# Channel mixing of a fused attention kernel: later loads of the second pass held to set times, planner durations a few per cent longer

## Chip, cores and metric

One NeuronCore of a Trainium2 chip runs the whole program. The metric is device microseconds (us) for one execution, lower is better. The kernel before takes 673.16 us (median of 3 runs, 673.02 to 673.44).

## Reference

Three blocks follow each other, on B=4 batches, H=8 heads, S=576 tokens, D=64, so C=512 channels and 2304 tokens.

```python
scores = where(mask, q @ k.T / sqrt(D), -1e9)   # window 32; heads 4..7 every 4th of 128
x = softmax(scores) @ v                         # B, S, C
# block 1, channel mixing
xk, xr = mu_k*x + (1-mu_k)*x_prev, mu_r*x + (1-mu_r)*x_prev
x = sigmoid(xr @ w_r) * (maximum(xk @ w_k, 0)**2 @ w_v)        # 512 -> 1024 -> 512
# block 2, token and channel mixing
u = x + (maximum(x.T @ w_tok1, 0) @ w_tok2).T                  # 576 -> 256 -> 576
out = u + maximum(u @ w_ch1, 0) @ w_ch2                        # 512 -> 1536 -> 512
```

## The kernel before

The program is written as one long list of steps (function `tile_model`), and nothing in the list is issued at once. A class `Plan` collects the steps and their dependencies, and `order` (L304) then plays them through in planned time: every step has a duration from `_cost` (L258), a due time that is worked back from the PE step that needs it, and the engine that comes free first takes the ready step with the earliest due time. `emit` (L407) writes the instructions in that order, all from L421. This is why all rows of the profile name L421; a row is told apart by its tiles. On the chip each engine runs its instructions in that order and waits on semaphores; planned times do not exist there.

Four things steer the planner around this change:

- `_cost` gives the planned duration of a transfer (SP, SyncE's queue, issues all of them), of an ACT and of a DVE instruction.
- Copies, conversions and some scalings are written with both engines (`nc.either`, L470). The planner takes the first named one, ACT for copies, unless that would end too late; then the one that ends sooner. So durations decide which engine does them.
- `nc.hold` gives a step an earliest planned time, counted from the time that PE would reach this place of the list if it never waited. The weights of the second pass have such holds (L1264), weight conversions too (`slowly`, L836).
- `SPARE` is added to the planned landing of a load when a step of `slowly` reads it.

Precision: every fp32 product is split in a high and a low part (fp32r) and done with three matmuls (`mm3`). The large products use seven-product block forms (names A11, S1, A12, S2, S4, S3, A22), so 2x2 blocks need seven sweeps.

The part that the holds touch is the last product, `out = u + mid @ w_ch2`. A first pass wrote `mid` (1536 channels) to DRAM as `part_mid0` to `part_mid2`, one for each c of three groups of 768 tokens, and u as `part_u0` to `part_u2`. The second pass, `result(c)` (L1276), does for each c:

- `load(q)` (L1280) fetches quarter q of `part_mid` as two tiles of 128x1152 into a ring of 14 places (`half_r`: tiles wv, raw, z, at); four loads of 128x768 fetch u into `us`.
- `parts(q)` splits a tile into high and low, 128x1152 each, on ACT or DVE; `turned` and `less` form differences of tiles on DVE.
- `sweep` runs one of the seven forms on PE: two banks, 18 matmuls of 384 columns each. S2, S4, S3 and A22 add into banks that hold an earlier sum.
- `plus` empties a bank on DVE into an output tile (128x384), `send` stores it to `outT` through SP. The output tiles are a ring of three: z4, z5 (their last third) and y0.

Each c gives eight output tiles. All loads of the next c may be issued by SP as soon as their place in the ring is free; the planner puts them among the stores and weight loads by due time. Before the second pass, SP also fetches the seven weight forms from DRAM (`part_A11` to `part_A22`), which the first pass's weight conversions stored there.

The early part, for the other terms: `keys`, `receptance` and `mix` are the products with w_k, w_r and w_v of block 1, run between the attention units of the first batches.

Of the kernel before, what the change touches and what calls it, by code (L numbers as in the profile page):

```python
# [154 lines left out]
class Plan:  # L155
# [17 lines left out]
    }  # L173
    TAIL = dict(tensor=0.0, vector=0.08, scalar=0.10, gpsimd=0.0, sync=0.0)
    TICK, BUSY = 10.24 / 3, 3060
    SPARE = 3.0

    def __init__(self, nc):
        self.nc = nc
# [77 lines left out]
    @staticmethod  # L257
    def _cost(engine, method, kw):  # L258

        out = kw["out"]  # L260
        cols = int(np.prod(out.shape[1:]))
        pointers = sum(hasattr(kw.get(k), "space") for k in ("scale", "bias", "scalar", "scalar1"))
        if engine == "sync":
            if kw["in_"].dtype == U32:
                return max(0.45, 4 * cols * out.shape[0] / 230e3 - 0.9)
            return max(0.45, 8 * (0.03 + 4 * cols * 0.0266e-3))
        if engine == "tensor":
            if kw.get("is_transpose"):
                return cols / 1200 + 0.0025
            if kw["lhsT"].dtype in (F32R, BF16):  # L270
                return cols / 2263 + 0.0049
            if kw["lhsT"].shape[0] <= D or out.shape[0] <= D:
                return cols / 1200 + 0.0025
            return 2 * max(cols / 1200 + 0.0025, 0.112)
        source = kw.get("in_", kw.get("in0"))
        psum = source is not None and "PSUM" in str(source.space)
        if engine == "scalar":
            read = 0.093 * (kw.get("accum_out") is not None)
            return (0.07 if psum else 0.1) + cols / 1200 + 0.03 * pointers + read
        if engine == "gpsimd":  # L280
            return 0.04 if method == "memset" else 0.04 + cols / 345
        if method == "tensor_reduce":
            return 0.066 + int(np.prod(source.shape[1:])) / 960
        if method == "reciprocal":
            return 0.066 + cols / 157
        fast = method in ("tensor_copy", "tensor_scalar", "tensor_scalar_add") and not psum
        return 0.066 + 0.05 * pointers + cols / (1920 if fast else 960)

    def _run(self, at, cost, kw):

# [13 lines left out]
    def order(self):  # L304
# [41 lines left out]
        for _ in range(n):  # L346
# [50 lines left out]
            for s in after[i]:  # L397
                for o in self.ops[s]:
                    spare = self.SPARE if e == "sync" and s in self.floor else 0.0
                    ready[s][o] = max(ready[s][o], end + self.TAIL[e] + self.DELAY[e][o] + spare)  # L400
# [34 lines left out]
def tile_model(nc, banks, kept_k, kept_1, kept_w, kept_u, kept_mid, units, cst, mu, w_k, w_v, w_r, w_t1, w_t2, w_c1, w_c2, outT):  # L435
# [40 lines left out]
    def combine(out, in0, in1, op):  # L476
        nc.vector.tensor_tensor(out=out, in0=in0, in1=in1, op=op)

    def split(raw, hi, lo):
        copy(hi, raw)  # L480
        combine(lo, raw, f(hi), ALU.subtract)

    def rows(n):
        return slice(128 * n, 128 * n + 128)
# [264 lines left out]
    def mix(c, m, j):  # L749
# [16 lines left out]
        out=om_sb, in0=mu_sb, scalar1=-1.0, scalar2=1.0, op0=ALU.mult, op1=ALU.add  # L766
    )
    diag = []
    for kt in range(4):
        diag.append([])  # L770
        for k, factor in enumerate((om_sb, mu_sb)):
# [3 lines left out]
                    out=d, in0=ident, scalar1=factor[:, col], scalar2=None, op0=ALU.mult)),  # L775
# [68 lines left out]
    for g in range(8 * nchunk + 2):  # L844
        c, m = divmod(g, 8)
# [34 lines left out]
    def product(out, a, b, first=True, last=True, goes_on=False):  # L880
        for k, ((ah, al), (bh, bl)) in enumerate(zip(a, b)):
            mm3(out, ah, al, bh, bl, first and k == 0, last and k == len(b) - 1, goes_on)
# [377 lines left out]
    for n, (name, places) in enumerate(zip(NAMES, w2_at)):  # L1260
        start = len(nc.ops)
# [14 lines left out]
    def result(c):  # L1276
        us = [u_r.tile(2, N2) for _ in range(4)]
        quads = {}

        def load(q):  # L1280
            quads[q] = [half_r.tile(3, N2) for _ in range(2)]
            for i, t in enumerate(quads[q]):
                nc.sync.dma_start(out=t, in_=kept_mid[c][:, q, 3 * i:3 * i + 3])

        def parts(q):
            out = []
            for t in quads[q]:
                hl = tuple(hl_r.tile(3, N2, dtype=F32R) for _ in range(2))
                split(t, *hl)
                out += [tuple(v[:, k] for v in hl) for k in range(3)]  # L1290
            return out

        def less(q, other):
            for t, o in zip(quads[q], quads[other]):
                combine(t, t, o, ALU.subtract)

        def turned(q, other):
            for t, o in zip(quads[q], quads[other]):
                combine(t, o, t, ALU.subtract)

        def sweep(name, b, banks, **kw):
            for a in range(2):
                lhs = [tuple(v[:, rows(a)] for v in hl) for hl in w2[name]]
                product(banks[a], lhs, b, **kw)

        def plus(ps, others, tiles):
            for p, o, t in zip(ps, others, tiles):
                combine(t, p, o, ALU.add)

        def send(tiles, kt, half):  # L1310
            for a, t in enumerate(tiles):
                at_t = 2 * N2 * c + N2 * half
                nc.sync.dma_start(out=outT[rows(kt + a), at_t:at_t + N2], in_=t)

        def two(r):
            return [r.tile(N2) for _ in range(2)]

        def u_of(kt, half):
            return [us[kt + a][:, half] for a in range(2)]

        x, y, z = two(x_r), two(y_r), two(z_r)
        on = dict(first=False, goes_on=True)
        load(0)
        load(1)
        for kt in range(4):
            nc.sync.dma_start(out=us[kt], in_=kept_u[c][:, kt])
        load(2)
        load(3)
        sweep("A11", parts(0), x)
        s1 = two(aside_r)  # L1330
        plus(x, u_of(0, 0), s1)
        turned(0, 1)
        sweep("S1", parts(0), y)
        s5 = two(aside_r)
        plus(y, u_of(2, 1), s5)
        sweep("A12", parts(2), z)
        t = two(out_r)
        plus(z, s1, t)
        send(t, 0, 0)
        turned(0, 3)  # L1340
        sweep("S2", parts(0), x, **on)
        s2 = two(aside_r)
        plus(x, u_of(0, 1), s2)
        sweep("S4", parts(3), y, **on)
        t = two(out_r)
        plus(y, s2, t)
        send(t, 0, 1)
        less(3, 1)
        sweep("S3", parts(3), x, **on)
        t = two(out_r)  # L1350
        plus(x, s5, t)
        send(t, 2, 1)
        less(2, 0)
        sweep("A22", parts(2), x, **on)
        t = two(out_r)
        plus(x, u_of(2, 0), t)
        send(t, 2, 0)

    for c in range(3):
        result(c)  # L1360
# [88 lines left out]
```

## Time and profile before

| | |
|---|---|
| runs, median (lowest to highest) | 673.16 us (673.02 to 673.44) |
| the profiled execution | 671.81 us |
| its span, first to last instruction | 670.0 us |
| PE busy, matmuls | 653.8 us, 98%, 4105 matmuls |
| DVE busy | 566.7 us, 85%, 1188 instructions |
| ACT busy | 371.4 us, 55%, 981 instructions |
| DMA | 146.45 MB, mean 219 GB/s |
| chain that ended last | PE 72%, DVE 11%, DMA 9%, ACT 5% |

A busy time says how long an engine had an instruction in hand, averaged over stages with different limits. PE at 98% means that only 16 us of the span are free of matmuls, 7.4 us of them in the first 50 us. The chain is followed back from the last instruction, at each step to whatever released it.

### The profile page before, as it was taken

Reading aid. Unit: us, or ns where it says so; the run is one execution under the profiler, and the core shown is the slowest. Engines: PE = TensorE matmul, PEld = TensorE weight load, DVE = VectorE, ACT = ScalarE, POOL = GpSimd, SP = SyncE. Lnnn points to the kernel's source line nnn. Section 1 sums busy time; section 2 is a strip of 40 time slices with the busy share of each in tenths; the row PEclk is TensorE's granted clock in tenths of the full one; section 3 lists DMA queues with packets and bytes.
Section 4 is the critical chain, followed back from the end, with each engine's and each line's share of the span. In section 5 each row is a group of like instructions: output and inputs, shape, how many; then the busy total and the mean of one; then the engine's idle time right before and its main releaser. Section 6 shows DMA issues by size and latency. Waiting matters only on the chain.

```text
span 670.0 us, 11558 instructions
## 1 busy us (share of the span) xinstructions
PE 653.8 (98%) x4105; PEld 603.0 (90%) x4105; DVE 566.7 (85%) x1188; ACT 371.4 (55%) x981; POOL 2.1 (0%) x22
## 2 busy tenths in 40 slices
PE   6899999999999999999999999999999999899997
PEld 6678888888888888998889899999999999899997
DVE  4999998799799989777699888798898569899982
ACT  4989785789669875435278555264474122312310
POOL 0000000000000000000000000000000000000000
PEclk9999999999999999999999999999999999999999
DMA  8989444675774535713533769777697999933211
GB/s 325 385 310 331 142 126 150 190 261 166 249 237 149 198 115 179 237 38 121 164 111 133 233 193 364 275 254 256 247 356 253 413 408 412 392 107 95 71 36 59
DMA packets 65385, 146.45 MB, mean 219 GB/s; under 512 B 5808, under 2 KB 24368, under 8 KB 64304
## 3 DMA queue, kind: packets, MB, share of 16 engines
q1 hardware_dynamic: 65328, 145.72, 62.3%
q8 instruction: 32, 0.52, 0.3%
q14 instruction: 25, 0.20, 0.1%
HBM read 95.89 MB, written 49.81 MB: 217 GB/s over the span
## 4 chain that ended last, share of the span: by engine, by line
PE 72%; DVE 11%; DMA 9%; ACT 5%; issue 1%; SPq 0%; DVEq 0%; ACTq 0%
PE bank L421 72%; DVE z L421 3%; DVE at L421 2%; DVE x L421 2%; DMA z<-part_mid 2%; ACT z L421 2%; DVE wv L421 1%; ACT at L421 1%; ACT x L421 1%; DMA outT<-z 1%; DMA outT<-y 1%; DMA x<-w_k 1%; DMA wr<-units 1%; DMA part_mid<-at 1%; DMA at<-units 1%
## 5 line engine op out<-in xcount | busy, mean ns | idle before, releaser
L421 PE MATMUL bank<-z,wk 128*128 128x384 f32 x644 | 141.9, 345 | 0.3 <-ACT z L421 0.3
L421 PE MATMUL bank<-wv,z 128*128 128x512 f32 x432 | 124.3, 402 | 1.3 <-ACT raw L421 1.3
L421 PEld LDWEIGHTS bank<-z,wk 128*128 128x128 f32 x644 | 112.7, 188 | 5.7 <-ACT z L421 0.9
L421 PEld LDWEIGHTS bank<-wv,z 128*128 128x128 f32 x432 | 78.0, 188 | 14.6 <-ACT raw L421 1.6
L421 ACT ACTIVATE at<-at 128x96 f32<-128x96 f32 (+3 forms) x183 | 67.0, 369 | 36.3 <-DVE at L421 34.9
L421 ACT ACTIVATE z<-z 128x384 fp32r<-128x384 f32 (+1 forms) x90 | 46.4, 523 | 23.2 <-DVE z L421 15.7
L421 PE MATMUL bank<-xt,wk 128*128 128x384 f32 x254 | 54.0, 346 | 0.8 <-ACT at L421 0.8
L421 PE MATMUL bank<-wr,z 128*128 128x512 f32 x192 | 53.7, 406 | 1.0 <-DVE z L421 1.0
L421 PE MATMUL bank<-xt,x 128*128 128x384 f32 x248 | 48.8, 334 | 0.0
L421 PE MATMUL bank<-z,x 128*128 128x384 f32 x232 | 47.0, 334 | 0.0
L421 PEld LDWEIGHTS bank<-xt,wk 128*128 128x128 f32 x254 | 44.4, 188 | 2.6 <-issue 1.1
L421 DVE TENSOR_TENSOR z<-z,z 128x384 fp32r<-128x384 f32 (+1 forms) x78 | 44.2, 574 | 1.8 <-ACT z L421 0.6
L421 PEld LDWEIGHTS bank<-xt,x 128*128 128x128 f32 x248 | 43.5, 188 | 0.0
L421 DVE TENSOR_TENSOR at<-bank,at 128x384 f32<-128x384 f32 x64 | 35.2, 552 | 7.8 <-PE bank L421 7.2
L421 PEld LDWEIGHTS bank<-wr,z 128*128 128x128 f32 x192 | 34.3, 188 | 7.3 <-DVE z L421 1.3
L421 PEld LDWEIGHTS bank<-z,x 128*128 128x128 f32 x232 | 40.8, 188 | 0.0
L421 ACT ACTIVATE x<-bank 96x512 f32<-96x512 f32 (+1 forms) x48 | 28.1, 589 | 11.8 <-PE bank L421 11.6
L421 ACT ACTIVATE at<-bank 128x384 f32<-128x384 f32 x36 | 17.5, 488 | 27.0 <-PE bank L421 26.2
L421 DVE TENSOR_TENSOR raw<-raw 128x256 f32<-128x256 f32 (+1 forms) x76 | 30.2, 420 | 0.2
L421 PE MATMUL bank<-at 128*128 128x96 f32 (+1 forms) x121 | 22.1, 275 | 5.4 <-DMA at<-cst 5.0
L421 PE MATMUL bank<-cst,at 128*96 128x128 f32 x144 | 26.8, 274 | 0.2 <-DVE at L421 0.2
L421 PE MATMUL bank<-z,at 128*128 128x512 f32 x96 | 25.5, 397 | 0.0
(234 smaller groups left out, 1327.1 us busy)
## 6 DMA issues: line engine op xcount, KB each, us to landing
part_mid<-at SPq DMA_DIRECT2D x18, 768.0 KB, 5.9
z<-part_mid SPq DMA_DIRECT2D x11, 576.0 KB, 9.3
x<-w_c SPq DMA_DIRECT2D x12, 512.0 KB, 4.0
at<-units SPq DMA_DIRECT2D x14, 416.0 KB, 3.7
unit<-units SPq DMA_DIRECT2D x13, 416.0 KB, 3.8
at<-units SPq DMA_DIRECT2D x21, 256.0 KB, 3.4
part_w<-wv SPq DMA_DIRECT2D x21, 256.0 KB, 2.7
part_w<-x SPq DMA_DIRECT2D x21, 256.0 KB, 3.0
```

The source lines that it names most:

```text
L421: call(kw["out"], kw["constant"]) if method == "memset" else call(**kw)
```

## The change

Three constants of the planner and one earliest time are changed; what is computed, and every step of the list, stays.

```diff
-    SPARE = 3.0
+    SPARE = 2.0
...
-            return max(0.45, 8 * (0.03 + 4 * cols * 0.0266e-3))
+            return max(0.45, 8 * (0.045 + 4 * cols * 0.0266e-3))
...
-            return (0.07 if psum else 0.1) + cols / 1200 + 0.03 * pointers + read
+            return (0.08 if psum else 0.11) + cols / 1170 + 0.03 * pointers + read
...
-        return 0.066 + 0.05 * pointers + cols / (1920 if fast else 960)
+        return 0.075 + 0.05 * pointers + cols / (1860 if fast else 930)
...
-        load(0)
-        load(1)
-        for kt in range(4):
-            nc.sync.dma_start(out=us[kt], in_=kept_u[c][:, kt])
-        load(2)
-        load(3)
+        for wait, first, q in ((-5.0, 0, 0), (-5.0, 0, 1), (0.0, 1, 0), (5.0, 0, 2), (5.0, 0, 3)):
+            start = len(nc.ops)
+            if first:
+                for kt in range(4):
+                    nc.sync.dma_start(out=us[kt], in_=kept_u[c][:, kt])
+            else:
+                load(q)
+            if c:
+                nc.hold.update(dict.fromkeys(range(start, len(nc.ops)), wait))
```

So for c=1 and c=2 the first four loads may start, in planned time, 5 us before the group's first matmul, u at it, and the last four 5 us after it. The number of transfers is the same (355), and PE has the same 4105 matmuls; 164 steps that either engine can do change theirs, 85 from DVE to ACT and 79 from ACT to DVE.

SP, from the last weight loads before the second pass to its start. A name like `x21_1_4077` is a tile of the slot x21; `part_S3_82` is the DRAM copy of weight form S3. Before:

```order
L421 DMA x26_1_3686<-part_S2_80 128x1024
L421 DMA part_mid2_89<-at0_2_4184 512x1x384
L421 DMA x20_1_3889<-part_S4_81 128x2048
L421 DMA x21_1_4077<-part_S4_81 128x1024
L421 DMA at0_2_4184<-part_u0_84 128x768
L421 DMA x21_1_4077<-part_S3_82 128x1024
L421 DMA x22_3_4130<-part_S3_82 128x1024
L421 DMA x23_3_4240<-part_S3_82 128x1024
L421 DMA wr0_3_5411<-part_A22_83 128x1024
```

and now:

```order
L421 DMA z1_3_5324<-part_mid0_87 128x1152
L421 DMA part_mid2_89<-at0_2_4186 512x1x384
L421 DMA raw0_2_3330<-part_u0_84 128x768
L421 DMA x20_1_3896<-part_S4_81 128x2048
L421 DMA at0_2_4186<-part_u0_84 128x768
L421 DMA x21_1_4082<-part_S4_81 128x1024
L421 DMA part_S3_82<-y0_3_4387 128x512
L421 DMA x21_1_4082<-part_S3_82 128x1024
L421 DMA x22_3_4123<-part_S3_82 128x1024
L421 DMA x23_3_4245<-part_S3_82 128x1024
L421 DMA wr0_3_5423<-part_A22_83 128x1024
```

A load of u (raw0) and a store to part_S3 come here from further up the queue (both stood in the 13 rows above), and the other load of u now precedes x21's. In those rows, too, the loads of S1's weights (wk1, wk2, 128x1024 and 128x2048) now precede a store to part_mid2 that stood ahead of them, and x26's load precedes those of z0 and z1.

SP, the rows that follow, around the first output stores; `part_mid1_88` and `part_u1_85` are c=1's data, z4 and z5 the output tiles. Before:

```order
L421 DMA z3_1_5420<-part_mid1_88 128x1152
L421 DMA wr1_3_5431<-part_A22_83 128x1024
L421 DMA wr3_3_5442<-part_A22_83 128x1024
L421 DMA z4_2_5438<-part_mid1_88 128x1152
L421 DMA z5_2_5461<-part_mid1_88 128x1152
L421 DMA at2_2_4135<-part_mid1_88 128x1152
L421 DMA outT<-z5_2_5461 128x384
L421 DMA at0_2_4184<-part_mid1_88 128x1152
L421 DMA outT<-z4_2_5438 128x384
L421 DMA at0_2_4184<-part_mid1_88 128x1152
L421 DMA wv0_2_3622<-part_mid1_88 128x1152 x2
L421 DMA unit0_2_4088<-part_u1_85 128x768
```

and now:

```order
L421 DMA wr1_3_5434<-part_A22_83 128x1024
L421 DMA wr3_3_5446<-part_A22_83 128x1024
L421 DMA outT<-z4_2_5442 128x384
L421 DMA outT<-z5_2_5461 128x384
L421 DMA z3_1_5481<-part_mid1_88 128x1152
L421 DMA z4_2_5442<-part_mid1_88 128x1152
L421 DMA z5_2_5461<-part_mid1_88 128x1152
L421 DMA at2_2_4134<-part_mid1_88 128x1152
L421 DMA unit0_2_4088<-part_u1_85 128x768
L421 DMA unit1_2_4108<-part_u1_85 128x768
L421 DMA outT<-y0_4_5526 128x384
L421 DMA at0_2_4186<-part_mid1_88 128x1152 x2
```

The first two output stores now precede all loads of c=1, and the c=1 loads of at0 and wv0 come behind those of u and a third output store. Further on, c=2's eight loads stood before among the stores of c=0; now four of them stand behind the store of z4 that SP issued at 600.87 in the profile, and four behind the next store of z5.

PE, around the second receptance product (`wr` by z0, z1); `wv0` by z4 are the mixing products. Before:

```order
L421 MATMUL bank0_63<-at0_0_339 128x96 x4
L421 MATMUL bank3_66<-wr2_1_507,z0_0_402 128x512 x3
L421 MATMUL bank3_66<-wr3_1_516,z0_0_402 128x512 x3
L421 MATMUL bank3_66<-wr0_1_438,z1_0_493 128x512 x3
L421 MATMUL bank3_66<-wr1_1_449,z1_0_493 128x512 x3
L421 MATMUL bank1_64<-cst0_0_111,at2_0_142 96x128 x4
L421 MATMUL bank5_68<-wv0_1_597,z4_1_547 128x512 x2
```

and now:

```order
L421 MATMUL bank0_63<-at0_0_366 128x96 x4
L421 MATMUL bank5_68<-wv0_1_587,z4_1_545 128x512
L421 MATMUL bank6_69<-wv0_1_587,z4_1_545 128x512
L421 MATMUL bank7_70<-wv0_1_587,z4_1_545 128x512
L421 MATMUL bank3_66<-wr2_1_505,z0_0_466 128x512 x3
L421 MATMUL bank3_66<-wr3_1_514,z0_0_466 128x512 x3
L421 MATMUL bank3_66<-wr0_1_429,z1_0_485 128x512 x3
```

Three mixing matmuls, which came later, stand ahead of the receptance rows. On ACT, five steps of the attention now precede the first conversion of w_k, and the first conversion of w_v precedes a step of `keys` that it followed.

## Rows read from the trace of the kernel before

**Rows 1.** The page, busy time, share of the span and instructions of each engine.
```profile
PE 653.8 (98%) x4105; PEld 603.0 (90%) x4105; DVE 566.7 (85%) x1188; ACT 371.4 (55%) x981; POOL 2.1 (0%) x22
```

**Rows 2.** Stretches (us): busy of PE, PEld, DVE, ACT, POOL; granted clock, DMA share, GB/s.
```profile
0.00:50.00 50.00, 42.59 (x357) 34.94 (x357) 39.55 (x93) 38.30 (x126) 1.08 (x20) 1.00 0.91 341
50.00:100.00 50.00, 49.02 (x386) 42.65 (x388) 49.48 (x106) 43.31 (x131) 0.00 (x0) 1.00 0.60 198
...
550.00:600.00 50.00, 47.94 (x275) 47.33 (x275) 45.84 (x49) 12.95 (x12) 0.00 (x0) 1.00 0.84 324
```

**Rows 3.** Timeline, PE: start, us, engine, operation, out<-in, count [idle before <-releaser].
```profile
50.92 3.06 PE L421 MATMUL bank<-wr,z 128*128 128x512 f32 x12 [0.96 <-DVE z L421]
...
572.21 5.02 PE L421 MATMUL bank<-xt,wr 128*128 128x384 f32 x25 [1.94 <-issue]
```

**Rows 4.** Timeline, DVE, before and in the second pass; same columns.
```profile
529.80 0.56 DVE L421 TENSOR_TENSOR at<-bank,at 128x384 f32<-128x384 f32 x1 [0.54 <-PE bank L421]
...
555.64 0.55 DVE L421 TENSOR_TENSOR z<-bank,at 128x384 f32<-128x384 f32 x1
...
565.89 1.36 DVE L421 TENSOR_TENSOR xt<-z,xt 128x1152 fp32r<-128x1152 f32 x1
568.43 0.56 DVE L421 TENSOR_TENSOR z<-bank,z 128x384 f32<-128x384 f32 x1 [1.18 <-DMA outT<-z]
568.90 1.35 DVE L421 TENSOR_TENSOR xt<-z,xt 128x1152 fp32r<-128x1152 f32 x1
570.28 1.36 DVE L421 TENSOR_TENSOR z<-z,z 128x1152 f32<-128x1152 f32 x1
571.56 0.55 DVE L421 TENSOR_TENSOR z<-bank,z 128x384 f32<-128x384 f32 x1
...
575.11 0.56 DVE L421 TENSOR_TENSOR y<-bank,z 128x384 f32<-128x384 f32 x1 [0.94 <-DMA outT<-y]
```

**Rows 5.** Timeline, SP's issues of transfers, before and in the second pass; same columns.
```profile
519.96 0.52 SPq L421 DMA_DIRECT2D part_mid<-at  x1
...
557.95 0.34 SPq L421 DMA_DIRECT2D outT<-z  x1
558.33 0.43 SPq L421 DMA_DIRECT2D at<-part_mid  x1
559.01 0.34 SPq L421 DMA_DIRECT2D outT<-z  x1
560.29 0.32 SPq L421 DMA_DIRECT2D at<-part_mid  x1
561.62 1.73 SPq L421 DMA_DIRECT2D wv<-part_mid  x2
564.55 1.75 SPq L421 DMA_DIRECT2D unit<-part_u  x2
566.52 0.34 SPq L421 DMA_DIRECT2D outT<-y  x1
...
600.87 0.34 SPq L421 DMA_DIRECT2D outT<-z  x1
```

**Rows 6.** Chain of waits: start, us, what.
```profile
557.95 8.51 DMA outT<-z
...
575.72 90.79 PE bank L421 x522
```

**Rows 7.** Stretch 560 to 570; columns as in rows 2.
```profile
560.00:570.00 10.00, 10.00 (x60) 9.95 (x58) 8.76 (x11) 1.17 (x1) 0.00 (x0) 1.00 1.03 411
```

**Rows 8.** Transfers issued at 536.07 and 537.29: count, KB, us to landing.
```profile
part_mid<-at SPq DMA_DIRECT2D x1, 768.0 KB, 11.7
...
x<-part_S SPq DMA_DIRECT2D x1, 1024.0 KB, 12.9
```

**Rows 9.** Timeline, ACT, first readers of c=1's and c=2's later loads.
```profile
579.17 1.17 ACT L421 ACTIVATE xt<-at 128x1152 fp32r<-128x1152 f32 x1 [0.34 <-PE bank L421]
...
610.38 1.17 ACT L421 ACTIVATE xt<-wv 128x1152 fp32r<-128x1152 f32 x1 [5.07 <-PE bank L421]
```

**Rows 10.** Timeline, ACT, first conversion of w_k.
```profile
24.79 1.15 ACT L421 ACTIVATE x<-x 128x1024 f32<-128x1024 f32 x1 [0.79 <-DMA x<-w_k]
```

## The prediction, made before the changed kernel had run

> **What bounds the kernel.** I read the page's engine table first: PE is busy 98% of the span, DVE 85% [rows 1]. So only the places where PE stands idle can be won. The table by stretches shows where they are [rows 2]: 7.4 us in the first 50 us, 1.0 in the next 50, where DVE is busy 49.5 of 50 us, and 2.1 in the stretch from 550 to 600. The granted clock is 1.00, the 2.4 GHz level, in every one of these rows, so no term below comes from the clock. The timeline of PE puts the late loss at one point: matmuls of sweep A22 start at 572.21 after 1.94 us of idle time [rows 3]. The page names no engine for it, so I followed the banks. A22 adds into bank 0, which DVE must first empty after sweep S3. DVE's timeline [rows 4] shows it late: it waits 1.18 us for a store of an output tile, starts at 568.43, then two passes over 128x1152 and, at 571.56, the row that empties bank 0; it ends at 572.11. A second wait, 0.94 us at 575.11 for the store of y, holds A22's later half: its matmuls start at 575.72 [rows 6], where 18 from 572.21 at 0.173 each (a sweep of 36 takes 6.24) would end near 575.4, so some 0.3 more.
>
> Why is that store late? The tile is written from 555.64 to 556.19 [rows 4], yet SP issues its store at 559.01 [rows 5]. It stands behind loads of the next 768 tokens, and SP cannot issue freely: the chain of waits [rows 6] shows the z5 store of 557.95 landing after 8.51 us, at 566.46, and SP issuing the y store at 566.52. Between these two issues lie exactly seven others [rows 5]. So **SP's ninth transfer waits until the first has landed**. With DMA at 103% and 411 GB/s [rows 7], each transfer lands when the bytes before it are through: 8 to 13 us after its issue.
>
> **The change, part by part.** It adds and removes no instruction. Hold times and costs act only in the planner; on the chip they are an order.
>
> 1. *The stores of the first output tiles, ahead of the loads.* In the new SP order the stores of z4 and z5 stand in front of z3, z4, z5 and at2 for c=1. I work out the landings by bytes at that rate: 0.64 us for a 128x512 store, 1.28 for a 128x1024 load, 1.43 for 128x1152, 0.96 for 128x768, 2.55 for 128x2048, 0.48 for an output tile. The starting point is the store of part_mid issued at 536.07, which landed 11.7 us later, at 547.8 [rows 8]. Two transfers, 0.64 + 0.96 us, no longer stand ahead of it, so it lands at 546.2. Behind it follow raw 0.96, x20 2.55, at0 0.96, x21 1.28 and the moved store to part_S3 0.64: 552.6. The load of x23 waits for that landing, since it reads what was stored; three loads of S3 and three of A22 take 7.7: 560.3. The two output stores land at 560.7 and 561.2, then z3 at 562.7, z4 at 564.1, z5 at 565.5, at2 at 567.0.
> DVE needs the z4 store by the end of its row of 565.89, which takes 1.27 start to start as the next ones do: 567.16. The store has landed 6.5 us earlier, so the 1.18 us wait goes. It then needs z3 at 567.6 and z5 at 568.9; both are there, z5 with 3.4 us to spare. Bank 0 is emptied from 570.2 to 570.8, 1.3 us sooner, and A22 starts at about 570.85. **What is late next** is DVE itself: PE could start at 570.27, so 0.6 of the 1.94 stays. The y store now lands near 569.4, before DVE's 573.8, so the 0.3 goes as well. Gain 1.3 + 0.3 = 1.6 us. The bounds: both stalls vanish, 2.2, or the work behind takes it all back, 0.
> 2. *Loads of c=1 and c=2 later.* The loads at +5 of c=1 (at0, wv) land by about 575, before the first row that reads them, ACT's of 579.17 [rows 9]. For c=2 the first four now stand behind stores of c=1, the last of them the one issued at 600.87 [rows 5]. They issue from 601.3 and land by bytes at 604.1 to 608.4; the first reader, ACT, started at 610.38 [rows 9]. Cost 0; the cover is 4 us or more, and each us beyond it would be a us of PE.
> 3. *SP before the second pass.* Loads of S1's weights pass the part_mid store of 519.96 [rows 5]: 1.57 MB less the raw load's 0.39 ahead of it, 2.9 us later, at 530.4. DVE's next write into that buffer was at 529.80 [rows 4], so DVE may wait 0.6. PE has other banks there: taken 0, bound 0.6. One weight load (x26, 1.28) now precedes the z0 and z1 loads, against 1.6 us taken away: 0.3 earlier, taken 0.
> 4. *The early order.* PE's three mixing matmuls (wv by z4, 512 columns) move ahead of the receptance row at 50.92, where it stood idle 0.96 [rows 3]. Twelve took 3.06 there, so three fill 0.7 or so. But on ACT the conversion of w_v, 128x1024 like ACT's row of 24.79 [rows 10] and so 1.0 us to the next start, now stands ahead of the step that this receptance row waits for through DVE: 1.0 later. Net +0.3; bounds -0.7 and +1.0. On ACT the first conversion of w_k waited 0.79 us for its load [rows 10]; five attention steps now fill that and 1.2 us more. Taken 0, since attention is that much further on; bounds -0.8 and +1.2.
> 5. *Engines.* By the new costs 85 steps go from DVE to ACT and 79 back; casts of 128x384 on DVE fall from 26 to 18, copies of it rise from 19 to 26. From 50 to 100, where DVE is the bound, PE has 1.0 idle to give back; I take half, -0.5, bounds -1.0 and +1.0 (one more wait like the one at 50.92). Between 100 and 550 PE idles little and DVE and ACT have room: 0, bounds of 1 either way.
>
> Sum: -1.6 + 0.3 - 0.5 = **-1.8 us**. The profiled execution took 671.81 (span 670.0 and 1.81 around it), so it would take 670.0; the runs' median, 673.16, is 1.35 above that execution, so I forecast 671.4.
>
> How much cover item 1 has hangs on the rate, 411 GB/s in the row. The Trainium skill, "DMA: Bandwidth & Descriptors", section Specifications, gives a limit of about 358 GB/s of HBM for each core; by it (an estimate from that page) the 7.9 MB from 546.2 to the landing of z5 would take 22.1 instead of 19.3 us, z5 would land at 568.4, half a us before its use, and the sum would be the same with its cover gone. The trace does not agree here; the measured rate stands.
>
> **The rivals.**
> *Nothing left (about 673.2).* The second pass gains its 1.6, and the early order loses as much: +1.0 at the receptance row and +0.6 of the 1.2 at w_k's conversion, with DVE too full from 50 to 100 to make it up. For it: those are the stretches with least slack. Against: PE's early idle time is mostly elsewhere. It is also the case in which the holds don't bind: nothing keeps SP from issuing on the chip but the order, and if DVE's own backlog alone set 572.21, earlier stores would change nothing. The 1.18 us in DVE's row speaks against that.
> *Slower by the moved store to part_S3 (675.5).* All weights of A22, both output stores and the loads of c=1 stand behind x23, which waits for this store. I have it issued at 547.2 and landing 5.4 us later. The store of 536.07 took 11.7 us and the load of 537.29 took 12.9 [rows 8]. z5 lands 12.9 us behind the store and A22 starts 1.95 us behind z5, so with a landing at 557.9 (10.7 us) the whole gain of item 1 is gone; from there each us is a us of PE. At 13.0 us z5 lands at 573.1, A22 starts at 575.0, 2.8 late, less 0.3 and 0.2 for the rest: +2.3. For it: the rows. Against: little is queued ahead at 547 (raw and x20, 3.5 us).
> *More than that (669.5).* The second pass gains the full 2.2, because DVE's run from 543 starts 0.3 earlier, and the early stretch gives 1.5 from the idle time above.
>
> **How the numbers follow.** Forecast case 0.5, nothing left 0.25, slower 0.15, more 0.1. A measurement of this kernel tells 0.2%, 1.35 us, from no change. The forecast and the larger gain count as faster (0.6), nothing left as the same (0.25), the rest as slower (0.15). The range takes in the larger gain with half a us, 669.0, and above 673.9, nothing left with 0.7 more from part of the bounds of items 3 to 5; the slower case stays outside.
>
> **What would show it.** Right: no wait for a store in DVE's row near 567; A22 starting near 570.9 with some 0.6 us of idle time, none 3.5 us later; SP issuing the z4 store at about 556.2; no wait for a load after 600. Wrong: an x23 load issued much after 552.6 or DVE waiting for z5 (the slower case); a wait of more than 1 us before the receptance row near 51, or PE's first 100 us longer than before by over 1 (nothing left).

## The result, and the profile after

Four runs of the changed kernel took 664.48 us in the median (664.06 to 664.57), four of the kernel before beside them 673.25 (673.02 to 673.44): ratio 0.987, 95% interval 0.985 to 0.989. The gain is 8.8 us where 1.8 was forecast, below the range. The profiled execution took 664.45 with a span of 662.7, so the spans differ by 7.3.

The page of the kernel after, busy time by engine, which answers to [rows 1]:

```profile
PE 651.1 (98%) x4105; PEld 603.0 (91%) x4105; DVE 562.1 (85%) x1182; ACT 379.4 (57%) x987; POOL 2.1 (0%) x22
```

PE does the same 4105 matmuls in 2.7 us less busy time and stands idle 4.6 us less. Stretches of the kernel before that the prediction did not show, with the columns of [rows 2]:

```profile
100.00:150.00 50.00, 49.61 (x337) 44.21 (x333) 42.39 (x113) 34.55 (x122) 0.00 (x0) 1.00 0.62 199
150.00:200.00 50.00, 48.73 (x356) 42.78 (x355) 44.42 (x123) 38.79 (x133) 0.00 (x0) 1.00 0.69 216
250.00:300.00 50.00, 49.92 (x257) 45.12 (x256) 41.86 (x95) 23.77 (x54) 0.00 (x0) 1.00 0.48 158
```

The same of the kernel after, with those of [rows 2] but the first:

```profile
50.00:100.00 50.00, 49.91 (x395) 43.46 (x394) 49.23 (x109) 45.20 (x137) 0.00 (x0) 1.00 0.64 216
100.00:150.00 50.00, 50.00 (x358) 44.56 (x358) 43.44 (x121) 35.87 (x128) 0.00 (x0) 1.00 0.62 197
150.00:200.00 50.00, 50.00 (x351) 44.74 (x348) 44.56 (x121) 38.73 (x127) 0.00 (x0) 1.00 0.73 229
...
550.00:600.00 50.00, 49.75 (x287) 49.46 (x286) 47.72 (x53) 12.88 (x11) 0.00 (x0) 1.00 0.66 243
```

PE is nearly gapless from 50 us on. But the table also hides something: between 100 and 550 the idle time falls only from 2.2 to 0.4 us, and PE got 3.9 ahead there. The rest does not show as idle time, since the ends of the matmuls are modelled: at token mixing, for one, idle time falls by 0.1 us, while 0.65 us less lies in distances from one matmul's start to the next that are 0.1 to 0.2 us longer than usual. So I compared starts: the matmul with the same number in both traces, at places where PE has done the same work in both. (The next matmul need not be the same one; at 50.92 it is the receptance row before and a mixing product after.)

| place in the program | before | after | earlier by |
|---|---|---|---|
| first attention work | 16.48 | 16.45 | 0.0 |
| before the receptance row of [rows 3] | 50.92 | 49.59 | 1.3 |
| block 1 | 100.41 | 99.08 | 1.3 |
| after the wait at 147 | 147.09 | 145.18 | 1.9 |
| after the wait at 162 | 162.50 | 159.06 | 3.4 |
| token mixing, start | 260.63 | 257.08 | 3.5 |
| token mixing, end | 293.03 | 288.60 | 4.4 |
| before the second pass | 504.45 | 499.36 | 5.1 |
| before S3's last part | 555.89 | 550.66 | 5.2 |
| A22, first bank | 572.21 | 565.29 | 6.9 |
| A22, second bank | 576.37 | 569.01 | 7.4 |
| last rows | 651.78 | 644.41 | 7.4 |

Three shares: **start-up 1.3, 100 to 550 us 3.9, second pass 2.1.** The forecast had 0.2, nothing and 1.6. The two waits in the middle are plain on PE's timeline of the kernel before (columns as in [rows 3]):

```profile
146.85 0.46 PE L421 MATMUL bank<-at 128*128 128x96 f32 x2 [0.39 <-DVE at L421]
...
162.50 0.71 PE L421 MATMUL bank<-wv,z 128*128 128x512 f32 x2 [1.27 <-ACT raw L421]
```

After, the same matmuls are inside groups without a wait, and the only waits of PE of 0.2 us or more that are left behind 20 us are three in the start-up, one of 0.29 at 396.68, which the kernel before has too (at 401.44), and one of 0.25 at A22:

```profile
24.79 0.88 PE L421 MATMUL bank<-xt,wk 128*128 128x384 f32 x2 [0.83 <-issue]
37.77 1.45 PE L421 MATMUL bank<-z,wk 128*128 128x384 f32 x5 [0.62 <-DVE z L421]
39.69 1.13 PE L421 MATMUL bank<-unit 128*128 128x96 f32 x8 [0.48 <-DVE at L421]
...
396.68 0.44 PE L421 MATMUL bank<-z,wk 128*128 128x384 f32 x1 [0.29 <-ACT z L421]
...
565.29 6.48 PE L421 MATMUL bank<-xt,wr 128*128 128x384 f32 x36 [0.25 <-issue]
```

For the second pass, SP's issues of the kernel after, which answer to [rows 5]:

```profile
541.79 0.43 SPq L421 DMA_DIRECT2D part_S<-y  x1
542.26 5.21 SPq L421 DMA_DIRECT2D x<-part_S  x3
547.52 1.39 SPq L421 DMA_DIRECT2D wr<-part_A  x3
550.57 2.07 SPq L421 DMA_DIRECT2D outT<-z  x2
552.69 1.60 SPq L421 DMA_DIRECT2D z<-part_mid  x3
...
592.41 0.33 SPq L421 DMA_DIRECT2D outT<-z  x1
592.80 0.91 SPq L421 DMA_DIRECT2D wv<-part_mid  x2
...
600.86 1.87 SPq L421 DMA_DIRECT2D z<-part_mid  x4
```

And DVE's rows there, for [rows 4]:

```profile
561.51 0.55 DVE L421 TENSOR_TENSOR z<-bank,z 128x384 f32<-128x384 f32 x1
561.98 1.35 DVE L421 TENSOR_TENSOR xt<-z,xt 128x1152 fp32r<-128x1152 f32 x1
563.36 1.36 DVE L421 TENSOR_TENSOR z<-z,z 128x1152 f32<-128x1152 f32 x1
564.64 0.55 DVE L421 TENSOR_TENSOR z<-bank,z 128x384 f32<-128x384 f32 x1
...
571.64 0.56 DVE L421 TENSOR_TENSOR z<-bank,raw 128x384 f32<-128x384 f32 x1 [1.39 <-DMA outT<-z]
```

The row that waited 1.18 us for a store, at 568.43 before, is the one at 561.51 here, without a wait; the two passes follow, and the row of 564.64 empties the bank that A22 needs. A wait for a store of 1.39 us comes two tiles later, at 571.64, where PE has nine matmuls of the next sweep running and loses nothing.

### The profile page after: what moved, and what is told of

Same layout as the page of the kernel before. It is cut to its first block, busy times and chain, and to the rows that moved or that the text cites. A ratio compares the mean times of both kernels' runs of the same rounds, so it can differ in the third digit from the quotient of the medians.

```text
span 662.7 us, 11575 instructions
## 1 busy us (share of the span) xinstructions
PE 651.1 (98%) x4105; PEld 603.0 (91%) x4105; DVE 562.1 (85%) x1182; ACT 379.4 (57%) x987; POOL 2.1 (0%) x22
## 4 chain that ended last, share of the span: by engine, by line
PE 91%; DMA 5%; DVE 2%; ACT 1%; issue 0%; SPq 0%; ACTq 0%
PE bank L421 91%; DMA wr<-units 2%; DMA unit<-units 1%; DMA raw<-w_v 1%; DMA wv<-units 1%; DVE x L421 1%; ACT z L421 0%; DVE wv L421 0%; DVE z L421 0%; DVE at L421 0%; ACT xt L421 0%; SPq L421 0%; DVE wr L421 0%; DVE unit L421 0%; ACT x L421 0%
## 5 line engine op out<-in xcount | busy, mean ns | idle before, releaser
L421 PE MATMUL bank<-wv,z 128*128 128x512 f32 x432 | 127.7, 404 | 0.0
L421 ACT ACTIVATE z<-z 128x384 fp32r<-128x384 f32 (+1 forms) x103 | 52.4, 520 | 25.2 <-DVE z L421 20.2
L421 PE MATMUL bank<-wv,x 128*128 128x384 f32 x132 | 24.8, 334 | 0.0
```

Of the source, the lines that this page charges most:

```text
L421: call(kw["out"], kw["constant"]) if method == "memset" else call(**kw)
```

## The experiments

**What was open.** The second pass moved as forecast; 3.9 us in the middle and 1.1 more in the start-up had no term. The theory after the first look: SPARE moves the loads that weight conversions read, and gives the middle; the durations give the start-up; the holds give the second pass. Rivals: the durations alone do it by moving steps between ACT and DVE, or it all hangs together.

### The parts alone

`e1_holds`: the kernel before with the holds, nothing else.

```diff
+        for wait, first, q in ((-5.0, 0, 0), (-5.0, 0, 1), (0.0, 1, 0), (5.0, 0, 2), (5.0, 0, 3)):
...
+                nc.hold.update(dict.fromkeys(range(start, len(nc.ops)), wait))
```

> Holds alone, constants as before: 0.3 us of the change is early order, so this differs from before in SP's queue of the second pass only. Theory A (the gains add, each where the trace shows it): the wait before sweep A22 falls from 1.9 us to about 0.4, the 0.3 before its later half goes; about 2.0 us off the time of before, 671.2; nothing changes ahead of 550. Theory B (the second pass also needs the moved weight and u transfers that only the new constants bring): the output stores still land late and under 1 us is won, 672.3 or more.

Measured 670.26 (669.39 to 671.77), ratio 0.996 (0.995 to 0.997): 3.0 us. A22 in its trace:

```profile
572.59 6.48 PE L421 MATMUL bank<-xt,wr 128*128 128x384 f32 x36 [0.89 <-issue]
```

0.89 instead of 1.94 us, and the second half without a wait: about 1.5 us in the trace, less than the 2.0 expected. Part of the rest of the 3.0 goes with the granted clock, which falls in fewer executions here; the comparison at equal clock stands under "Adding up". The order of the holds differs from that of before only on SP, from its 305th transfer on, so nothing ahead of the second pass can be theirs.

`e2_constants`: the change without its holds.

```diff
-    SPARE = 3.0
+    SPARE = 2.0
...
+            return max(0.45, 8 * (0.045 + 4 * cols * 0.0266e-3))
...
+            return (0.08 if psum else 0.11) + cols / 1170 + 0.03 * pointers + read
...
+        return 0.075 + 0.05 * pointers + cols / (1860 if fast else 930)
```

> All new constants, no holds. Theory A: PE's waits at 147 and 162 of before are gone as in the changed kernel, its start-up is 1 us shorter, but a wait of some 2 us before sweep A22 comes back, since in its SP queue the z4 store again stands behind loads of c=1: about 2 us above the changed kernel, 666.5. Theory B: as fast as the changed kernel within 0.7 us, since the constants also bring the second pass forward.

Measured 668.60 (666.99 to 669.57), ratio 0.994 (0.992 to 0.996): 4.6 us. Its wait at A22 is longer than before's, and DVE's row says why:

```profile
568.02 8.07 PE L421 MATMUL bank<-xt,wr 128*128 128x384 f32 x36 [3.27 <-issue]
```

```profile
564.24 0.56 DVE L421 TENSOR_TENSOR z<-bank,z 128x384 f32<-128x384 f32 x1 [2.63 <-DMA outT<-z]
```

PE comes to the second pass 5 us earlier, but the loads and stores there land at DMA's rate (its busy share is 1.01 to 1.02 from 545 to 565), so the constants lose part of their gain at A22. The sweep itself takes 8.07 us instead of 6.48, since the granted clock fell to half in it. Neither theory had this: 666.5 was the higher of the two. The holds are worth 3.0 alone and about 4 on top of the constants (668.6 to 664.5).

`e3_durations` and `e4_spare`: one half of the constants each.

```diff
 # e3_durations: the three lines of _cost, SPARE stays 3.0
 # e4_spare
-    SPARE = 3.0
+    SPARE = 2.0
```

> The longer durations of DVE, ACT and DMA alone, SPARE 3.0 and no holds. Theory A, first form (the early waits went because the planner now counts DVE and ACT as slow as they are): waits at 147 and 162 gone, start-up 1 us shorter, 666.5 to 668. Second form (they went because SPARE lets weight conversions start 1 us earlier): start-up shorter, but the waits near 150 to 165 stay: 670 to 672.

> SPARE 2.0 alone. First form: the waits near 147 and 162 stay, 672.5 to 673.5, start-up unchanged because its order is the same up to about 80 us. Second form: those waits go and 2 us are won, 671.

The durations took 673.00 (671.32 to 674.9), ratio 1.000 (0.998 to 1.002): nothing. SPARE took 669.14 (668.27 to 671.25), ratio 0.994 (0.993 to 0.996): 4.1 us. The second form was right for SPARE in kind, at twice the size; for the durations neither was, as both had a gain. The durations alone are no idle part, though: their PE is 1.7 us ahead at 51 us (0.3 of it by 13 us) and 3.9 at 162, and then loses 8.8, more than all of it, at one place (PE, and the chain of waits):

```profile
269.50 0.44 PE L421 MATMUL bank<-raw,wv 128*128 128x384 f32 x1 [0.32 <-DVE raw L421]
270.83 1.14 PE L421 MATMUL bank<-raw,wv 128*128 128x384 f32 x5 [0.90 <-DVE raw L421]
277.85 1.97 PE L421 MATMUL bank<-x,wk 128*128 128x384 f32 x5 [4.66 <-DVE x L421]
```

```profile
268.88 7.87 DMA part_w<-x
...
276.84 0.97 DVE x L421
...
277.85 12.22 PE bank L421 x51
```

A converted weight's store (`part_w<-x`) must land before DVE may write its tile again for token mixing. That conversion is the last of w_ch1's, and it is late. The clock fell with the wait (last columns but two: granted clock):

```profile
275.00:280.00 5.00, 2.15 (x7) 2.03 (x8) 2.44 (x6) 0.80 (x2) 0.00 (x0) 0.69 0.61 195
280.00:285.00 5.00, 5.00 (x21) 5.00 (x20) 3.30 (x8) 1.20 (x3) 0.00 (x0) 0.62 0.43 140
```

**Why SPARE reaches so far.** w_ch1 comes in twelve loads (`x<-w_c`, 512 KB), all into one buffer, a ring of one place: load, conversion on ACT and DVE, place free, next load. SPARE stands between landing and conversion, in every link, and so it adds up. The line of code (it stands in the cut of `e12_spare_w_c1` below) reaches further than the "planned landing of a load": it adds SPARE behind every transfer that a step of `slowly` waits for, and so also behind the stores `part_w` and `part_k`, whose tiles the conversions write again. SP's issues of the twelve loads, in us:

| load | before | durations | SPARE 2.0 | holds, SPARE 2.0 | after | after with SPARE 1.0 | SPARE 2.0 for w_ch1 alone |
|---|---|---|---|---|---|---|---|
| 1st | 78.08 | 76.61 | 79.02 | 78.31 | 76.98 | 78.12 | 78.16 |
| 4th | 131.30 | 126.98 | 128.86 | 128.17 | 126.68 | 127.38 | 127.63 |
| 8th | 184.38 | 180.18 | 177.69 | 176.98 | 176.00 | 174.68 | 179.45 |
| 12th | 244.97 | 242.12 | 233.02 | 232.32 | 233.12 | 225.29 | 239.04 |

The first and the last of them, before and in `e4_spare`:

```profile
78.08 0.38 SPq L421 DMA_DIRECT2D x<-w_c  x1
...
244.97 0.38 SPq L421 DMA_DIRECT2D x<-w_c  x1
```

```profile
79.02 0.38 SPq L421 DMA_DIRECT2D x<-w_c  x1
...
233.02 0.38 SPq L421 DMA_DIRECT2D x<-w_c  x1
```

From first to last the chain takes 166.9 us before and 154.0 with SPARE 2.0, about 1.2 less for each of eleven links. The last store of a converted piece (`part_w<-x`) goes out at 256.1 instead of 267.5, so ACT and DVE have the conversions behind them 11 us earlier, ahead of token mixing, and at 270 to 278 the pile-up of the durations is not there.

### Moving single steps by hand

These four ask whether the single waits that I saw are what a few displaced steps cost. The edits act on the finished order, on the kernel before for the first three, on the durations alone for the last. They add four lines, so the rows of these runs name L425.

```diff
-        for i in self.order():
+        sequence = self.order()
+        for i, j in ((267, 320), (268, 320)):              # e5_exp_first
+            sequence.remove(i)
+            sequence.insert(sequence.index(j), i)
+        for i in sequence:
...
+        # e6_mix_first: (1676, 1246), (1600, 1818), (1680, 1247), (1684, 1249)
+        # e7_both_and_holds: the six pairs, and the holds
+        # e8_durations_store_early: (2013, 2779), (2014, 2779), (2015, 2816)
```

> Before, with one move by hand: on ACT two exponentials of the attention go ahead of the first conversion of w_k, which waits for its load there. Theory C (the start-up gain is this order, and in most executions of before PE's wait at that place also brings a stretch of half clock, as in the profile of the run with holds alone): PE's wait on ACT near 27 (0.8 to 2.1 us) goes, no half clock from 27 to 30, 671.3 to 672 against 673.2. Rival (the conversion of w_k leads the chain, so what is won ahead of it is lost behind it): 673 or more, PE's first 60 us not shorter.

672.42 (671.4 to 674.17), ratio 1.000 (0.998 to 1.001). Two exponentials ahead of the first conversion of w_k on ACT: PE no longer waits for ACT at 27 us, but twice for DVE behind it.

```profile
30.15 0.64 PE L425 MATMUL bank<-cst,at 128*96 128x128 f32 x4 [0.33 <-DVE at L425]
32.09 0.64 PE L425 MATMUL bank<-cst,at 128*96 128x128 f32 x4 [0.43 <-DVE at L425]
```

Won ahead, lost behind: one wait of the start-up is not worth its length.

> Before, with four moves by hand on DVE: the steps of the mixing and keys products that PE waits for at 162.5 go ahead of five steps of a weight conversion that nobody waits for then. Theory D (DVE's order alone makes the wait at 162.5): 1.3 to 1.5 us off, 671.8, no wait of PE from 150 to 200. Rival (DVE is full there, so a later PE step waits as long): no gain, 673, a wait of about 1 us some 5 to 15 us later.

675.02 (673.18 to 676.43), ratio 1.003 (1.002 to 1.005): slower. With the mixing steps pulled ahead on DVE the wait at 162.50 was gone, and a longer one came 3 us later:

```profile
165.59 0.69 PE L425 MATMUL bank<-x,at 96*64 96x64 f32 x16 [2.50 <-ACT x L425]
```

My theory that a few misplaced steps cost the 1.3 us fell. Between 145 and 170 us of the kernel before DVE is busy 96% of the time and ACT 94%, and here whatever went ahead pushed attention back. The granted clock fell behind this wait, too; its mean from 165 to 170 is 0.73. That SPARE helps by bringing conversions of that stretch earlier fits the table above; a run with only these moved was not made.

> Before with the holds and the moves of both hand-made orders, planner constants as before. If the three gains lie at separate places and add: 673.2 less 3.0 (holds as measured), less 1.5, less 1.4, so 667.3; what the changed kernel has beyond that (664.5) then comes from 250 to 300 and from the rest of the early order. If they overlap: 668.5 or more.

673.54 (671.4 to 675.76), ratio 1.001 (1.000 to 1.002): the loss at 165 us came with it (2.49 us), and took what the holds gave (0.88 left at A22).

> Longer durations alone (673.0), with one move by hand: the last two conversion steps of tile x23 on DVE and their store go ahead of a step that waits 3.7 us for PE. Theory E (the durations' gain of 3 to 4 us ahead of 170 is lost in one place, because x23 is rewritten only after this store has landed): PE's wait of 4.7 us at 277.9 and the half clock from 277 to 284 go; 666.5 to 668.5. Rival (the wait at 277.9 has another cause, DVE's whole backlog there): 672 or more, the wait stays over 2 us.

672.69 (670.38 to 673.83), ratio 0.999 (0.998 to 1.001). The store was moved ahead, and PE still waited:

```profile
271.99 1.14 PE L425 MATMUL bank<-raw,wv 128*128 128x384 f32 x5 [1.46 <-DVE raw L425]
276.85 1.82 PE L425 MATMUL bank<-x,wk 128*128 128x384 f32 x5 [2.51 <-DVE x L425]
```

4.66 became 2.51 and 0.90 became 1.46, so the store was half of it at most, and the clock still fell there. DVE's own steps are late there too; which of them would have to go first was not tried.

### Adding up, and the chain by itself

`e9_after_again` is the changed kernel, `e10_holds_and_spare` the change without its durations, `e11_spare_1` the changed kernel with SPARE 1.0, `e12_spare_w_c1` the kernel before with 2.0 for the loads of w_ch1 only.

```diff
 # e10_holds_and_spare: the three lines of _cost as before
 # e11_spare_1
-    SPARE = 2.0
+    SPARE = 1.0
 # e12_spare_w_c1, in the planner, where the landing is planned
                     spare = self.SPARE if e == "sync" and s in self.floor else 0.0
+                    if spare and getattr(kw["in_"], "name", "") == "w_c1":
+                        spare = 2.0
```

> The changed kernel itself, once more, beside the three runs below on the same chip. Expected 664.5 (664 to 665.5), ratio to the kernel before 0.985 to 0.990, no PE wait over 1 us between 60 us and the end. If the small gap between medians and spans (8.8 against 7.3 us) was chance and not the clock, the gain here would be nearer 7.3 and the time nearer 666.

664.91 (663.46 to 666.95), ratio 0.988 (0.986 to 0.990) to the 673.07 of before: 8.2 us. Its profiled execution has a span of 661.9 and the same shape (PE ahead by 1.3 more at 51 us than at 16, 2.1 more at 162, 2.4 more over A22).

> The holds and SPARE 2.0 with the old durations. If the parts add (SPARE alone took 4.1 off, the holds alone 3.0), 673.2 - 7.1 = 666.1, and what the durations give in the changed kernel is the rest, some 1.6 us in the first 60 us, where PE's waits at 27 to 33 us must stand here again. Rival: the durations matter later too, because they steer the middle of the first pass; then this one is at 667.5 or above, with PE waits between 60 and 500 us that the changed kernel hasn't. A second rival: the durations give nothing on top (alone they gave 0.2), and this one is at 664.5.

666.85 (666.35 to 667.57), ratio 0.991 (0.989 to 0.992): 6.2 us, where 7.1 would be the sum of the two parts. The rest, 1.9 us, is what the durations give in the changed kernel. In its trace the wait of the receptance row stands again, while the waits expected at 27 to 33 do not:

```profile
51.16 3.02 PE L421 MATMUL bank<-wr,z 128*128 128x512 f32 x12 [0.98 <-DVE z L421]
```

So the durations' share is the start-up, and in part the wait at 162 (PE gains 1.4 there without them, 2.1 with them). One pair of traces says little on the size in the start-up: in the six profiles with the new durations the matmul at 50.92 of before starts 0.2 to 2.0 us earlier than there, in the five others with the old early order 0.1 to 1.0 later. The share counts only because SPARE has cleared the place at 270 us where the durations alone lost it again.

> The changed kernel with SPARE 1.0 in place of 2.0. By the chain through the one buffer x22, a further 1 us leaves each of its links: the last of the twelve loads goes out some 9 to 11 us earlier again, at about 223 us in place of 233. What that is worth depends on whether PE still waits there: in the changed kernel's profile PE has no wait over 0.3 us between 60 and 500, so the theory expects at most 0.5 us more gain, 664.0 to 665. Rival: 2 us was what the loads need; with 1 the converting steps stand in front of ACT and DVE before their loads have landed, what is queued behind them waits, and the kernel is slower than the changed one by 1 to 5 us, with PE waits between 80 and 260 us on DVE or ACT.

664.01 (663.01 to 665.91), ratio 0.987 (0.985 to 0.989): not to be told from the changed kernel. The twelfth load went out 8 us earlier again, at 225.29, and nothing came of it, as PE had no wait left there. Nor did a conversion stand in front of an engine before its load had landed.

> The kernel before with SPARE 2.0 for the twelve loads of w_c1 alone; all other loads keep 3.0. If the chain through x22 is what pays, most of the 4.1 us of SPARE 2.0 for all loads is here too: 669 to 670.5, with the waits at 147 and 162 us gone or below 0.7. Rival: the loads of the other weights, which are ahead of w_c1 on the same engines, matter as much; then less than half of it is here (671.3 to 673.2), the later links of the chain fall back to the old distance, and the waits at 147 and 162 stand.

670.32 (669.32 to 671.59), ratio 0.996 (0.994 to 0.997): 2.8 of the 4.1 us. The waits at 147 and 162 shrank as with SPARE for all loads (PE gains 1.3 at 162 against 1.4), but the chain's last links fell back (239.04), and of the 0.9 us at token mixing only 0.2 came. So the chain through one buffer carries most of it. The rest must be the other transfers that SPARE bears on: up to token mixing these are, in the main, the stores of converted pieces (`part_w`, `part_k`), and behind it w_ch2's loads. That is read from the code; no run has them alone.

**At equal clock.** Each execution comes with its mean granted clock. In the profiles 0.999 or 1.000 goes with no fall between start and end, 0.997 or less with one to three falls. Executions at 0.999 or more alone, those of the kernel before from all three sets beside the experiments, those of the changed kernel from both:

| kernel | at 0.999 or more | median | less than before |
|---|---|---|---|
| before | 28 of 73 | 672.0 | |
| holds | 10 of 12 | 669.9 | 2.1 |
| SPARE 2.0 | 5 of 8 | 668.8 | 3.2 |
| SPARE 2.0 for w_ch1 alone | 5 of 6 | 670.2 | 1.8 |
| holds, SPARE 2.0 | 4 of 5 | 666.7 | 5.3 |
| changed kernel | 8 of 9 | 664.5 | 7.5 |

Here the parts add: 2.1 and 3.2 are 5.3, and the durations give 2.2 on top. The durations alone have no execution to compare, as all ten are at 0.997 or less. The groups are small, down to four.

## Why the prediction was wrong

**Read right: the second pass, item 1.** The step held nearly to the number. Seen from PE, the changed kernel is 5.2 us earlier at that place; with this added back, the moved store to part_S3 lands 5.4 us after its issue, as forecast; the x23 load goes out at 552.4 (forecast 552.6), the z4 store is issued at 555.8 (556.2), and A22 starts at 570.5 (570.85). The wait at A22 is 0.25 in the row against the 0.6 that was to stay. "What is late next is DVE itself" was right: from 540 on no DVE row waits for a store or a load ahead of A22. The gain is 2.1 (1.7 at the first bank, 0.4 at the second), and the term had 1.6 (1.3 and 0.3), its upper bound being 2.2. The 0.4 more at the first bank is the start of DVE's run, which waits for a load of c=0 before and after:

```profile
543.29 0.76 DVE L421 CAST wv<-z 128x1152 fp32r<-128x1152 f32 x1 [5.43 <-DMA z<-part_mid]
```

```profile
537.65 0.76 DVE L421 CAST wv<-z 128x1152 fp32r<-128x1152 f32 x1 [6.17 <-DMA z<-part_mid]
```

That is 5.6 us earlier, where PE is 5.2 earlier; the rival "more than that" had 0.3 of it. On top of the constants the holds are worth about 4, because without them the constants' earlier PE would wait 3.3 us here; the term was priced against a PE that comes as late as before.

The cover of item 1 hung on the rate. The trace moved 383 GB/s on average from 540 to 565 and up to 438 in its slices, and z4, z5 of c=1 were there in time. The Trainium skill, "DMA: Bandwidth & Descriptors", section Specifications, has about 358 for each core; the trace of after does not agree either.

**Right: items 2 and 3.** c=1's later loads and c=2's eight cost nothing: PE has no wait of 0.2 us or more behind 565.29. c=2's first four went out right behind the store of z4 (592.41, the one of 600.87 before), as I had it. No wait of PE shows just ahead of the second pass.

**Wrong, and the step that failed: item 5, "Between 100 and 550 PE idles little and DVE and ACT have room: 0, bounds of 1 either way".** 3.9 us came from there. Three things in that sentence failed. PE did not idle little: the table by stretches had 2.2 us there, with one wait of 1.27, and as much again in gaps that the table counts as busy; a bound of 1 was below what the rows showed. DVE and ACT had no room where it mattered: an average of 0.85 to 0.89 busy between 100 and 200 us goes with a DVE that is busy 96% from 145 to 170. And **SPARE had no term at all**: the title names durations and holds, and the sum prices those. A constant that stands in each of twelve links of one chain is worth eleven times its size in when the chain ends. SPARE alone gave 4.1 us (3.2 at equal clock).

**Wrong in size and counted twice: items 4 and 5, start-up.** Item 4 had +0.3 net at the receptance row; the wait of 0.96 there went wholly and nothing came for it: the conversion of w_v that I saw ahead of a step of keys did not delay it. Item 5's half of "1.0 idle from 50 to 100" was that same wait: 50 less 49.02 is 0.98, and the row at 50.92 has 0.96 of it. Together -0.2 was forecast and 1.3 gained, in this pair of profiles.

**Wrong: "no term below comes from the clock", and with it the 1.35 added at the end.** The granted clock was 1.00 in all stretches of the one profile that I had. In 45 of the 73 executions of the kernel before it fell somewhere, and their median is 673.6 against 672.0 for the other 28. So most of the 1.35 by which the median lay above the profiled execution was the clock, and I carried it over to the changed kernel, where it fell in one execution of nine. At equal clock the change is worth 7.5 us, as the spans say (7.3); about 1 of the 8.8 is that such executions have become rare. That the removed waits are the reason fits the last section and is not shown by itself.

**The rivals.** Slower by the moved store to part_S3: it did not occur, as the store took 5.4 us and not 11. Nothing left: no. More than that had the right sign and the second pass right (2.2), but again only the start-up as its other source. No rival had the middle.

## What to carry to other kernels

When a planner's margin changes, look for a chain that runs through one buffer and count its links: load, convert, free, load again turns 1 us of margin into 11 at the end of the chain, and what this moves lies far from the edited line. Read gaps by the start of the same instruction in both traces: a busy share of nearly 100% hid 2 us here. And a part that measures nothing alone can be worth 2 us beside another that clears the place where it was given back.

## What the runs showed of the hardware that I had not expected

A PE wait can cost more than its length. In several executions the granted clock fell from 1.0 to half (1.2 GHz) shortly after a wait of PE, here in `e1_holds` (PE's rows, then the stretches):

```profile
27.41 2.90 PE L421 MATMUL bank<-xt,wk 128*128 128x384 f32 x4 [2.08 <-ACT at L421]
```

```profile
20.00:25.00 5.00, 4.20 (x68) 3.44 (x68) 4.08 (x13) 3.32 (x16) 0.00 (x0) 1.00 1.04 395
25.00:30.00 5.00, 2.92 (x8) 1.25 (x5) 3.34 (x7) 4.49 (x15) 0.00 (x0) 0.70 1.01 381
30.00:35.00 5.00, 5.00 (x75) 3.90 (x76) 4.81 (x9) 4.48 (x12) 0.17 (x2) 0.95 0.98 319
```

The same early order ran in six profiles: the clock fell near 27 us in three of them (holds, SPARE 2.0, mix first), behind waits of 2.08, 0.89 and 1.73 us, and not in the other three (before, holds with SPARE, SPARE for w_ch1), where the wait there was 0.81 or less. It fell at A22 behind waits of 3.27, 2.39 and 2.10 us, not behind 1.94 (before) or 1.81 (SPARE 2.0); near 165 behind 2.50 and 2.49 (`e6_mix_first`, `e7_both_and_holds`); and at 277 in `e8_durations_store_early` behind 2.51 and in `e3_durations` behind 4.66, where the same matmuls fell 2.3 us further behind between 277.85 and 283.77. So not every such wait brings it, a length that brings it at one place does not at another, and the same kernel can have it in one execution and not in the next. The changed kernel's two profiles have none.
